# Key products of two chunks by pairs, two chunks of scores moved into the loop, and seven constant products ahead of it

## The chip, the cores and the metric

The kernel runs on one core of one Trainium2 chip. The metric is the device time of one execution in microseconds (us), as a median over runs. The profile is one further execution, recorded by the hardware profiler; it has a time of its own, and all rows below come from it. The engines are TensorE (PE in the rows; PEld is its weight load), VectorE (DVE), ScalarE (ACT), GpSimd (POOL) and SyncE (SP), which issues most DMAs.

## The reference, cut to what matters

A gated delta rule over 768 tokens for 4 batches of 8 heads (head size 48), and after it a mixture of 16 experts of which every token takes one:

```
k_n = k / (norm(k) + 1e-6)
for t in range(S):
    y[t]  = q[t] @ state                        # state: 48 x 48 for each batch and head
    v_old = k_n[t] @ state
    state = state + beta[t] * outer(k_n[t], v[t] - v_old)
x = y as 3072 rows of 384
group, then expert in the group, by argmax;  out = gate * (relu(x @ w1[e]) @ w2[e])
```

## The kernel before, in words

The 768 tokens are worked on in 24 chunks of 32 tokens (u = 0 to 23). Four chunks form a group. For each chunk `gram(u)` multiplies the chunk's keys by its keys and by its queries (one product for each pair of a batch and a head, in tiles of 48 rows by 32 columns) and ScalarE moves the results to SBUF: `gt` (keys by keys) for the group's inverse, `gq` (keys by queries, the raw scores) for the chunk. A product in f32 runs as two passes on TensorE, so 32 products stand as x32 in the order of instructions and as x64 in the trace; the transposes by the identity run as one pass each.

`inverse(g)` is the long part on VectorE: it turns `gt` over (L297), takes the norms, and inverts 32 by 32 triangles by some 90 small products and sums (L367, L373), then turns the result back (L401) and spreads it into `mtb` (L410 on VectorE, L412 on ScalarE). Only when `mtb` of group 0 is there can the first `w` be made (L488), and with it the recurrence begins.

The recurrence has one period for each chunk: `w_ps` (L488), state products `s_ps` (L499), the state copied back by ScalarE (`s_bd`, L505), output products `o_ps` (L513), then with the new state `a_ps` (L471) and `o_ps` of the next chunk (L480), a transpose of the finished rows (`t_ps`, L540), and `f` (L475), which `w_ps` of the next period reads. In each period `gram(u + 10)` stands between `w_ps` and `s_ps`, so that scores are made 10 chunks ahead (`LEAD = 10`). VectorE meanwhile goes on with the inverse of a later group; `scale(u + 2)` (L448) makes `vh` from the values `kv`.

The order of the work is written out by hand: within the attention part PE, DVE, ACT, POOL and SP each run their instructions in program order. Ahead of the loop the grams of chunks 0 to 9 are made. The first twelve steps are key products of chunks 0 to 3, both products of chunks 4 to 7, and query products of chunks 0 to 3; their PSUM homes change between a tile `g_ps` and two tiles `begin0`, `begin1`. Chunks 8 and 9 come after them, then two products of constants (L817) into the tile `s_ps`, which takes over the banks of `begin0` and `begin1`. Loads are timed by touches: ScalarE writes one column of a tile (L784), and the load of that tile on SP (L199 for keys and queries, L203 for values, L209 for constants) has to wait for it. The constants come in two parts; the second (`con`, 376.5 KB) holds the identity that the constant products read.

After period 23 the mixture of experts runs, 16 experts one after the other, bound by TensorE.

Of the kernel before, what the change touches and what calls it, by code (L numbers as in the profile page):

```python
# [9 lines left out]
F32 = mybir.dt.float32  # L10
I32 = mybir.dt.int32
AX = mybir.AxisListType
ALU = mybir.AluOpType
# [3 lines left out]
C = 32  # L17
RG = 4
# [48 lines left out]
def deltanet_then_moe(  # L67
# [109 lines left out]
    with ExitStack() as first:  # L177
# [59 lines left out]
        gts, raws, gqs, mts, norm, vhs, xs, turned_over = {}, {}, {}, {}, {}, {}, {}, set()  # L237
        begun_with = {}

        def gram(u, home=None, parts=(0, 1)):  # L240


            g, uu = divmod(u, RG)
            kqt = kqt_[u % NB]
            if uu == 0 and 0 in parts:
                gts[g] = wk.tile([128, C, RG, H], F32, tag="gt", name=f"gt{g}")
            g_ps = home
            if home is None:
                g_ps = ps.tile([128, 2, 512], F32, tag="g", name=f"g_ps{u}")
            g_out = g_ps.rearrange("p f (j x) -> p (f j) x", j=NP)[:, :, 0:2 * C].rearrange(  # L250
                "p h (a t) -> p h a t", a=2)
            for j in range(NP):
                for b in range(B):
                    for hh in range(2):
                        rows = slice(hh * 64, hh * 64 + D)
                        of = slice(parts[0], parts[-1] + 1)
                        nc.tensor.matmul(g_out[quads[b], hh * NP + j, of],  # L257
                                         lhsT=kqt[rows, 0, j, quads[b]],
                                         rhs=kqt[rows, of, j, quads[b]], start=True, stop=True,
                                         skip_group_check=True)  # L260
            if 0 in parts:
                nc.scalar.activation(
                    gts[g][:, :, uu].rearrange("p t h -> p h t"), g_out[:, :, 0, :],
                    ACT.Copy)
            if 1 not in parts:
                return None
            raws[u] = wk.tile([128, H, C], F32, tag="gq", name=f"gq{u}", bufs=LEAD + 1)
            nc.scalar.activation(raws[u], g_out[:, :, 1, :], ACT.Copy)
# [19 lines left out]
        def inverse(g):  # L288
# [30 lines left out]
                yield ROOTS  # L319
            else:  # L320
                nc.scalar.activation(r0, diag, ACT.Sqrt, bias=cut["tiny"])
                nc.scalar.activation(rooted, cut["tiny"], ACT.Exp)
                yield BEGUN
                nc.vector.reciprocal(r1, r0)
                yield
# [428 lines left out]
        def work(n):  # L754


            for task in behind:
                if held.get(task) not in (TURN, ROOTS, FACTOR):
                    due[task] = min(due[task] + n * 180 * rate[task], 4000.0)
            while True:  # L760
                able = [t for t in behind if held.get(t) is None and due[t] > 0]
                if not able:
                    break
                for task in able:
                    push(task)

        def allow(what):

            for task in list(behind):
                if held.get(task) is what:  # L770
                    push(task)
# [5 lines left out]
        with tc.manual_schedule(engines={mybir.EngineType.PE, mybir.EngineType.DVE,  # L777
# [3 lines left out]
            def begin(burst):  # L781

                for late, loads in burst:
                    nc.scalar.activation(late[:, 0:1], cut["tiny"], ACT.Copy)  # L784
                    for load in loads:
                        load()
# [1 line left out]
            first_grams = ([(u, (0,)) for u in range(RG)] + [(u, (0, 1)) for u in range(RG, 2 * RG)]  # L788
                           + [(u, (1,)) for u in range(RG)])
            for i, (u, parts) in enumerate(first_grams):  # L790
                gram(u, homes[i % len(homes)], parts)
                begin(bursts.get(i, ()))
                if i == RG - 1:
                    start(inverse(0), 1)
                    while BEGUN not in held.values():
                        work(2)
            allow(BEGUN)
            work(22)
            for _ in range(6):
# [3 lines left out]
            nc.gpsimd.tensor_copy(what[:, :, 0:2], cut["ids"].rearrange("p (u c) -> p u c", c=2))  # L803
            nc.gpsimd.tensor_copy(sel, ident.rearrange("p (g r) -> p g r", r=BL)[:, :, None, :]
                                  .to_broadcast([128, 4, 4, BL]))
            ahead = advance(0)
            next(ahead)
            for u in range(2 * RG, LEAD):
                gram(u, homes[u % len(homes)])
                begin(after_gram[u])  # L810
            begin_with.close()
            pst = first.enter_context(tc.tile_pool(name="ps_state", bufs=1, space=PSUM, side="right"))
            s_ps = pst.tile([128, B, 512], F32, tag="state", name="s_ps")
            s_at = s_ps[:, :, 0:H * D].rearrange("p b (j d) -> p b j d", j=NP)
            sorted_in.update(at=s_ps[:, 0, H * D:H * D + T * 3 * NE], begun=True)
            for n in (H * D, H * D):
                nc.tensor.matmul(s_ps[:, 0, 0:n], lhsT=ident, rhs=con[:, cols[1]:cols[1] + n],  # L817
                                 start=True, stop=True, skip_group_check=True)
            second = inverse(1)
            start(second, 0.95)  # L820
            while 0 not in mts:
                work(4)
                allow(ACT_STEP)
            mask(0)
            scale(1)
            allow(ROOTS)
# [1 line left out]
                work(2)  # L828
            allow(FACTOR)
            ahead_of = {u: [u + LEAD] if u + LEAD < NCH else [] for u in range(NCH + 1)}  # L830
            begun, x_in = set(), {}

            def add_rows(j, **how):
# [43 lines left out]
            for u in range(NCH + 1):  # L877
# [44 lines left out]
                if ending:  # L922
# [1 line left out]
                        allow(SORT)  # L924
                    found_0 = read_found()
                    gathered = gather_first(found_0)
                for v in ahead_of[u]:
                    gram(v)
                if ahead_of[u] or later or ending:
                    next(step)  # L930
# [9 lines left out]
                if not ahead_of[u] and not later and not ending:  # L940
                    next(step)
                next(step)
                if u < NCH - 1:
                    allow(PE_STEP)
                    allow(ACT_STEP)
# [383 lines left out]
```

## Time and profile before

| | |
|---|---|
| time, median of 3 runs | 493.04 us (491.14 to 493.22) |
| the profiled execution's own time | 492.32 us |
| its span, first to last instruction | 490.6 us |
| busy share of the span | PE 91%, PEld 86%, DVE 48%, ACT 40%, POOL 39% |
| mean granted TensorE clock | 0.992 |
| first `w_ps` begins | 42.01 us |
| `w_ps` of periods 1 and 2 | 49.71 and 56.82 us |

A timeline row reads: start in us, duration in us, engine, line, operation, output<-inputs, shape, xcount of instructions merged in the row, and in brackets how long the engine stood idle before it and what released it. "issue" as releaser means that nothing in the profile (no semaphore, no DMA) held the engine. A row with SPq is SP's queue issuing a DMA. In the DMA view, q1 carries the loads and stores of the program and q8 carries instructions.

### The profile page before, as it was taken

To read this page: it belongs to the slowest core of one execution; us is meant where nothing else is said; L and a number is where in the kernel's file an instruction comes from. 1 tells how busy PE (TensorE), PEld (TensorE's weight loads), DVE (VectorE), ACT (ScalarE), POOL (GpSimd) and SP (SyncE) were. 2 spreads that over 40 slices of the span, in tenths; PEclk is the share of its full clock that TensorE was granted. 3 is DMA by queue.
4 is the path that set the end of the run, shared out by engine and by line. 5 is a ranking of instruction groups with operands and counts; after the bars stand their busy time and mean duration, and the time that the engine had idled before them with its cause. 6 is when DMAs were issued, how large, how long until landed. Compare 5 with 4: busy or idle time off the path is not lost. (4 is left out here: it accounts for less than half of the span.)

```text
span 490.6 us, 18139 instructions
## 1 busy us (share of the span) xinstructions
PE 447.1 (91%) x7738; PEld 422.6 (86%) x7738; DVE 236.1 (48%) x866; ACT 193.8 (40%) x415; POOL 188.9 (39%) x328
## 2 busy tenths in 40 slices
PE   3437999999999999999999999999999999999992
PEld 3325888888888888889999999999999999999992
DVE  2998999999999994465201201220122012201210
ACT  3416978798887766641112112111211111111110
POOL 0041210634517132102466355544645465265122
PEclk9999999999999989999999999999999999999998
DMA  5466454454356533106978877967977797878830
GB/s 165 141 193 190 154 168 146 131 173 149 93 165 179 180 106 106 59 22 171 364 227 252 277 255 204 310 181 246 339 260 234 270 330 276 253 221 305 278 112 31
DMA packets 56741, 97.07 MB, mean 198 GB/s; under 512 B 18958, under 2 KB 41417, under 8 KB 56659
## 3 DMA queue, kind: packets, MB, share of 16 engines
q1 hardware_dynamic: 50739, 85.89, 54.7%
q0 software_dynamic: 5920, 10.00, 6.7%
q8 instruction: 62, 1.02, 0.9%
q14 instruction: 20, 0.16, 0.1%
HBM read 81.75 MB, written 14.27 MB: 196 GB/s over the span
## 5 line engine op out<-in xcount | busy, mean ns | idle before, releaser
L1113 PE MATMUL y_ps<-hid,w 128*128 128x224 f32 (+15 forms) x768 | 132.2, 331 | 0.0
L1113 PEld LDWEIGHTS y_ps<-hid,w 128*128 128x128 f32 x768 | 129.0, 190 | 0.3
L1094 PE MATMUL h_ps<-xt,w 128*128 128x232 f32 (+14 forms) x720 | 122.7, 330 | 0.0
L1094 PEld LDWEIGHTS h_ps<-xt,w 128*128 128x128 f32 x720 | 120.1, 190 | 0.3
L1066 POOL DMA_INDIRECT xq<-x_dram,from_q x92 | 87.6, 953 | 37.0 <-issue 24.6
L1097 ACT ACTIVATE hid<-h_ps 128x448 f32<-128x448 f32 (+15 forms) x64 | 32.1, 502 | 100.2 <-PE h_ps L1094 100.2
L1116 DVE COPY yt<-y_ps 128x232 f32<-128x232 f32 (+13 forms) x14 | 5.1, 366 | 135.3 <-PE y_ps L1113 135.3
L1125 POOL DMA_INDIRECT out_dram<-yo,to_i x32 | 34.0, 1064 | 91.3 <-DVE yo L1163 80.3
L1118 ACT ACTIVATE yt<-y_ps 128x224 f32<-128x224 f32 (+15 forms) x34 | 11.5, 337 | 116.6 <-PE y_ps L1113 116.6
L373 DVE TENSOR_TENSOR m<-m,below 128x16 f32<-128x16 f32 (+4 forms) x180 | 53.8, 299 | 0.3
L367 DVE TENSOR_TENSOR below<-m 128x16 f32<-128x16 f32 (+4 forms) x180 | 52.5, 293 | 0.1
L505 ACT ACTIVATE s_bd<-s_ps 48x768 f32<-48x768 f32 x46 | 37.0, 805 | 6.0 <-PE s_ps L499 5.1
L1163 DVE TENSOR_SCALAR yo<-yr,gate 128x384 f32<-128x384 f32 (+14 forms) x28 | 11.1, 415 | 48.5 <-DMA yr<-y_dram 39.8
L257 PE MATMUL g_ps<-kqt 48*32 48x64 f32 (+1 forms) x1216 | 19.4, 236 | 15.3 <-issue 7.9
L257 PEld LDWEIGHTS g_ps<-kqt 48*32 48x32 f32 x1216 | 14.8, 116 | 17.8 <-issue 12.9
L488 PEld LDWEIGHTS w_ps<-f,mtb 64*64 64x64 f32 x736 | 23.7, 137 | 5.6 <-ACT f L475 3.8
L412 ACT ACTIVATE mtb<-mt,con 128x256 f32<-128x256 f32 x39 | 28.2, 747 | 0.0
L488 PE MATMUL w_ps<-f,mtb 64*64 64x48 f32 x736 | 26.6, 222 | 1.5 <-ACT f L475 1.4
L499 PE MATMUL s_ps<-w,kv 32*112 32x96 f32 x736 | 24.5, 267 | 1.2 <-issue 0.5
L499 PEld LDWEIGHTS s_ps<-w,kv 32*112 32x112 f32 x736 | 20.5, 172 | 3.8 <-ACT w L492 0.8
L471 PE MATMUL a_ps<-s_bd,kqt 112*32 112x96 f32 x736 | 21.2, 253 | 2.3 <-ACT s_bd L505 1.3
L592 POOL TENSOR_TENSOR acc<-acc,hots 128x16 f32<-128x16 f32 x16 | 4.2, 261 | 47.1 <-DVE hots L590 46.1
(176 smaller groups left out, 577.2 us busy)
## 6 DMA issues: line engine op xcount, KB each, us to landing
w<-in_w_dram SPq DMA_DIRECT2D x29, 1536.0 KB, 8.8
kv<-in_kv_dram SPq DMA_DIRECT2D x24, 416.0 KB, 3.6
kqt<-in_kq_dram SPq DMA_DIRECT2D x20, 448.0 KB, 4.1
x_dram<-x SPq DMA_DIRECT2D x24, 192.0 KB, 2.3
w<-in_w_dram SPq DMA_DIRECT2D x24, 128.0 KB, 3.9
y_dram<-yq SPq DMA_DIRECT2D x36, 84.0 KB, 9.0
yr<-y_dram SPq DMA_DIRECT2D x14, 192.0 KB, 2.4
kqt<-in_kq_dram SPq DMA_DIRECT2D x8, 224.0 KB, 3.9
```

Of the source, the lines that this page charges most:

```text
L257: nc.tensor.matmul(g_out[quads[b], hh * NP + j, of], lhsT=kqt[rows, 0, j, quads[b]], rhs=kqt[rows, of, j, quads[b]], start=True, stop=True ...
L367: nc.vector.tensor_tensor(t, column.to_broadcast(like), row.to_broadcast(like), op=ALU.mult)
L373: nc.vector.tensor_tensor(to, to, t, op=ALU.add)
L412: nc.scalar.activation(mtb[:, rows, a], from_, ACT.Copy, scale=by)
L488: nc.tensor.matmul(w_ps[b, h], lhsT=mt[b, uu * H + (h % 2) * NP + h // 2], rhs=f[b, h], start=(h == 0), stop=True, skip_group_check=True)
L499: nc.tensor.matmul(s_at[0:KR, b, j], lhsT=k[quads[b], j, 0:KR], rhs=w[quads[b], 2 * j:2 * j + 2], start=(u == 0 and j == 0), stop=True, sk ...
L505: nc.scalar.activation(s_bd[rows, :, :, hh, :], s_at[rows, :, :, hh * D:(hh + 1) * D], ACT.Copy)
L1066: nc.gpsimd.indirect_dma_start(out=xq[:, g, :], out_offset=None, in_=x_dram[:, :].rearrange("n (q c) -> (n q) c", q=4), in_offset=bass.Ind ...
L1094: nc.tensor.matmul(h_ps[:, k], lhsT=w1[:, j, (f + k) * 128:(f + k + 1) * 128], rhs=xt[:, j, 0:R], start=(j == 0), stop=(j == DC - 1), skip ...
L1097: nc.scalar.activation(hid[:, f:f + 2], h_ps, ACT.Relu)
L1113: nc.tensor.matmul(y_ps, lhsT=w2[:, f, j * 128:(j + 1) * 128], rhs=hid[:, f], start=(f == 0), stop=(f == FC - 1))
L1125: put = nc.gpsimd.indirect_dma_start(out=out[:, :], out_offset=bass.IndirectOffsetOnAxis(ap=to[0:P, i:i + 1], axis=0), in_=yo[0:P, :], in_ ...
```

## The change: what it does

Three edits, and two small moves that go with them.

- `gram` has a new form `paired`, used for the first two steps (key products of chunks 0 and 1). Two batches are multiplied at once: 16 products of 64 by 64 in place of 32 of 32 by 32. Of each result the two blocks on the diagonal are wanted; ScalarE takes the even one times a mask into `part`, and VectorE adds the odd one times its mask into `gt`.
- The grams of chunks 8 and 9 leave the stretch ahead of the loop. Period 0 now makes chunks 8 and 9, period 1 makes chunks 10 and 11, each the first between `w_ps` and `s_ps` and the second after `o_ps`. From period 2 on it is as before.
- The two constant products become seven.
- The load of the exponential's table on ScalarE (the second ACT_TABLE_LOAD) moves from just after the square root to after all first grams.
- The touches that start the loads of chunks 10, 11, 12 and of the values of chunk 2 move behind the spreading of `mtb` of group 0. The first step of `advance(0)` moves with the products.

```diff
+            if paired:
+                for j in range(NP):
+                    for b in pairs:
+                        for hh in range(2):
+                            k = kqt[hh * 64:hh * 64 + D, 0, j, b]
+                            nc.tensor.matmul(g_out[b, hh * NP + j], lhsT=k, rhs=k, start=True,
+                                             stop=True, skip_group_check=True)
+                even, odd = cut["parity"][:, 0:1], cut["parity"][:, 1:2]
+                part = wk.tile([128, H, C], F32, tag="part", name=f"part{u}")
+                nc.scalar.activation(part, g_out[:, :, 0], ACT.Copy, scale=even)
+                nc.vector.scalar_tensor_tensor(
+                    gts[g][:, :, uu].rearrange("p t h -> p h t"), in0=g_out[:, :, 1], scalar=odd,
+                    in1=part, op0=ALU.mult, op1=ALU.add)
+                return
...
-                nc.scalar.activation(rooted, cut["tiny"], ACT.Exp)
...
-                gram(u, homes[i % len(homes)], parts)
+                gram(u, homes[i % len(homes)], parts, i < 2)
...
+            nc.scalar.activation(rooted, cut["tiny"], ACT.Exp)
...
-            for u in range(2 * RG, LEAD):
-                gram(u, homes[u % len(homes)])
-                begin(after_gram[u])
...
-            for n in (H * D, H * D):
+            for n in [H * D] * 7:
...
             while 0 not in mts:
                 work(4)
                 allow(ACT_STEP)
+            for u in range(2 * RG, LEAD):
+                begin(after_gram[u])
...
+            ahead_of.update({u: [2 * RG + 2 * u, 2 * RG + 2 * u + 1] for u in range(2)})
...
-                for v in ahead_of[u]:
+                for v in ahead_of[u][:1]:
                     gram(v)
...
                 next(step)
+                for v in ahead_of[u][1:]:
+                    gram(v)
```

On PE, from the last of the first twelve grams to the second `w_ps`, before (the number after a tile's name is the chunk; L257 is a gram):

```order
L257 MATMUL begin1_104<-kqt3_108 32x32 x32
L257 MATMUL begin1_104<-kqt8_113 32x64 x32
L257 MATMUL g_ps9_761<-kqt9_114 32x64 x32
L817 MATMUL s_ps_805<-con_66 128x384 x2
L488 MATMUL w_ps0_882<-vh0_715,mtb0_854 64x48 x16
L257 MATMUL g_ps10_903<-kqt10_115 32x64 x32
L499 MATMUL s_ps_805<-w0_899,kv0_117 112x96 x16
L513 MATMUL o_ps0_720<-w0_899,gqm0_857 64x48 x16
L471 MATMUL a_ps1_901<-s_bd_99,kqt1_106 32x96 x16
L480 MATMUL o_ps1_1048<-s_bd_99,kqt1_106 32x96 x16
L540 MATMUL t_ps0_1067<-con_66,x0_986 128x128 x3
L488 MATMUL w_ps1_1086<-f1_1046,mtb0_854 64x48 x16
```

and now (L271 is a gram, L826 the constant products, L501 `w_ps`):

```order
L271 MATMUL begin1_104<-kqt3_108 32x32 x32
L826 MATMUL s_ps_696<-con_66 128x384 x7
L501 MATMUL w_ps0_787<-vh0_687,mtb0_751 64x48 x16
L271 MATMUL g_ps8_809<-kqt8_113 32x64 x32
L512 MATMUL s_ps_696<-w0_804,kv0_117 112x96 x16
L526 MATMUL o_ps0_704<-w0_804,gqm0_762 64x48 x16
L271 MATMUL g_ps9_894<-kqt9_114 32x64 x32
L484 MATMUL a_ps1_806<-s_bd_99,kqt1_106 32x96 x16
L493 MATMUL o_ps1_990<-s_bd_99,kqt1_106 32x96 x16
L553 MATMUL t_ps0_1009<-con_66,x0_892 128x128 x3
L501 MATMUL w_ps1_1028<-f1_988,mtb0_751 64x48 x16
```

Two grams have left the stretch ahead of `w_ps0`, five constant products have come into it, and period 0 has one gram more, between `o_ps0` and `a_ps1`.

On ACT, from the last query scores of the first twelve grams to `w0`, before (L262 and L268 empty a gram, L784 is a touch, L412 spreads `mtb`):

```order
L268 ACTIVATE gq3_585<-begin1_104 128x256
L262 ACTIVATE gt2_721<-begin1_104 128x8x32
L268 ACTIVATE gq8_755<-begin1_104 128x256
L784 ACTIVATE kqt10_115<-con_66 128x1
L784 ACTIVATE kv2_119<-con_66 128x1
L262 ACTIVATE gt2_721<-g_ps9_761 128x8x32
L268 ACTIVATE gq9_795<-g_ps9_761 128x256
L784 ACTIVATE kqt11_116<-con_66 128x1
L784 ACTIVATE kqt0_105<-con_66 128x1
L412 ACTIVATE mtb0_854<-mt0_852,con_66 128x8x32
L492 ACTIVATE w0_899<-w_ps0_882 128x384
```

and now (L282 empties a gram, L797 is a touch, L425 spreads `mtb`, L810 is the moved table load):

```order
L282 ACTIVATE gq3_556<-begin1_104 128x256
L810 ACT_TABLE_LOAD
L810 ACTIVATE rooted_130<-con_66 128x1
L425 ACTIVATE mtb0_751<-mt0_749,con_66 128x8x32
L797 ACTIVATE kqt10_115<-con_66 128x1
L797 ACTIVATE kv2_119<-con_66 128x1
L797 ACTIVATE kqt11_116<-con_66 128x1
L797 ACTIVATE kqt0_105<-con_66 128x1
L505 ACTIVATE w0_804<-w_ps0_787 128x384
```

The spreading no longer stands behind four gram evictions, and the four touches stand behind it, together.

On ACT in period 0, from the first gram's eviction to `f` of the next period, before:

```order
L262 ACTIVATE gt2_721<-g_ps10_903 128x8x32
L268 ACTIVATE gq10_937<-g_ps10_903 128x256
L505 ACTIVATE s_bd_99<-s_ps_805 48x16x48 x2
L522 ACTIVATE x0_986<-o_ps0_720 128x384
L412 ACTIVATE mtb0_854<-mt0_852,con_66 128x8x32 x2
L475 ACTIVATE f1_1046<-a_ps1_901 128x384
```

and now (L518 copies the state, L535 the output, L488 makes `f`):

```order
L276 ACTIVATE gt2_808<-g_ps8_809 128x8x32
L282 ACTIVATE gq8_843<-g_ps8_809 128x256
L518 ACTIVATE s_bd_99<-s_ps_696 48x16x48 x2
L535 ACTIVATE x0_892<-o_ps0_704 128x384
L276 ACTIVATE gt2_808<-g_ps9_894 128x8x32
L282 ACTIVATE gq9_928<-g_ps9_894 128x256
L425 ACTIVATE mtb0_751<-mt0_749,con_66 128x8x32 x2
L488 ACTIVATE f1_988<-a_ps1_806 128x384
```

Two more evictions stand ahead of `f1`. In period 1 two stand ahead of `f2` in the same way. SP's and POOL's instructions stand in the same order as before.

## Rows read from the trace of the kernel before

**Rows 1.** The page's second part: the span in 40 equal slices of 12.3 us, the busy share of each in tenths.

```profile
PE   3437999999999999999999999999999999999992
...
DVE  2998999999999994465201201220122012201210
```

**Rows 2.** The timeline of PE from the start to period 2; counts are passes.

```profile
3.56 0.89 PE L257 MATMUL g_ps<-kqt 48*32 48x32 f32 x64 [3.56 <-DMA kqt<-in_kq_dram]
5.50 1.55 PE L257 MATMUL begin<-kqt 48*32 48x32 f32 x128 [1.05 <-DMA kqt<-in_kq_dram]
6.84 0.53 PE L257 MATMUL g_ps<-kqt 48*32 48x32 f32 x31
9.22 0.49 PE L257 MATMUL g_ps<-kqt 48*32 48x32 f32 x33 [1.84 <-issue]
11.18 1.97 PE L257 MATMUL begin<-kqt 48*32 48x64 f32 x94 [1.47 <-DMA kqt<-in_kq_dram]
14.51 0.85 PE L257 MATMUL begin<-kqt 48*32 48x64 f32 x34 [1.35 <-issue]
...
34.12 0.66 PE L257 MATMUL begin<-kqt 48*32 48x32 f32 x37 [5.27 <-issue]
...
38.34 0.88 PE L257 MATMUL g_ps<-kqt 48*32 48x64 f32 x38 [1.52 <-issue]
39.16 2.93 PE L817 MATMUL s_ps<-con 128*128 128x384 f32 x4
42.01 1.17 PE L488 MATMUL w_ps<-vh,mtb 64*64 64x48 f32 x32
...
44.48 0.33 PE L257 MATMUL g_ps<-kqt 48*32 48x64 f32 x12 [0.61 <-issue]
...
56.82 1.13 PE L488 MATMUL w_ps<-f,mtb 64*64 64x48 f32 x32
```

**Rows 3.** The DMA queues (queue and kind: packets, MB, share of 16 engines). First the page's row of q8 over the whole span, then the stretch 35.8 to 38.4 us (where q1 has no packet), then 38.3 to 41.8 us (where q8 has none), then 41.8 to 43.2 us.

```profile
q8 instruction: 62, 1.02, 0.9%
...
q8 instruction: 1, 0.02, 2.3%
...
q1 hardware_dynamic: 285, 0.95, 96.8%
...
q8 instruction: 1, 0.02, 4.9%
```

**Rows 4.** The timeline of VectorE: group 0's `gt` turned over, the first `vh`, group 0's result turned back, the last step ahead of the third `vh`, and that `vh`.

```profile
10.45 1.25 DVE L297 STREAM_TRANSPOSE m<-gt 128x1024 f32<-128x1024 f32 x1 [7.96 <-ACT gt L262]
...
28.95 0.56 DVE L448 TENSOR_TENSOR vh<-kv,normt 128x384 f32<-128x384 f32 x1
...
35.73 1.25 DVE L401 STREAM_TRANSPOSE mt<-m 128x1024 f32<-128x1024 f32 x1
...
41.16 0.21 DVE L373 TENSOR_TENSOR m<-m,corner 128x52 f32<-128x52 f32 x1
43.23 0.56 DVE L448 TENSOR_TENSOR vh<-kv,normt 128x384 f32<-128x384 f32 x1 [1.86 <-PE w_ps L488]
```

**Rows 5.** Loads and who reads them: SP's queue issues the values of chunk 0 and of chunk 2; POOL's first reading of the constants' second part; and, from the view of line L448 up to 60 us, the times at which VectorE's queue got through the two semaphore events of that line (the first of them is the one ahead of the third `vh`).

```profile
24.88 0.35 SPq L203 DMA_DIRECT2D kv<-in_kv_dram  x1
...
37.88 0.38 SPq L203 DMA_DIRECT2D kv<-in_kv_dram  x1
...
30.74 0.22 POOL L803 COPY what<-con 128x48 f32<-128x48 f32 x1 [15.30 <-DMA con<-in_const_dram]
...
L448 DVEq EVENT_SEMAPHORE  x2: 21/21/21, 42.8 to 51.3; - x2
```

**Rows 6.** The timeline of ScalarE: the second table load, the touches of chunks 6 and 7, the spreading ahead of the first `w`, and period 0 from its gram's eviction to `f`.

```profile
12.10 1.28 ACT L322 ACT_TABLE_LOAD   x1
...
14.20 0.28 ACT L784 ACTIVATE kqt<-con 128x1 f32<-128x1 f32 x2
...
40.17 0.73 ACT L412 ACTIVATE mtb<-mt,con 128x256 f32<-128x256 f32 x1
...
44.88 0.63 ACT L262 ACTIVATE gt<-g_ps 128x256 f32<-128x256 f32 x1 [0.64 <-PE g_ps L257]
45.30 0.43 ACT L268 ACTIVATE gq<-g_ps 128x256 f32<-128x256 f32 x1
...
47.50 0.49 ACT L522 ACTIVATE x<-o_ps 128x384 f32<-128x384 f32 x1
47.88 1.40 ACT L412 ACTIVATE mtb<-mt,con 128x256 f32<-128x256 f32 x2
49.19 0.47 ACT L475 ACTIVATE f<-a_ps 128x384 f32<-128x384 f32 x1
```

**Rows 7.** The stretch of the periods: the windows view from 45 to 170 us (stretch; its length; busy us and instruction count of PE, PEld, DVE, ACT, POOL; granted clock; DMA share; GB/s), what VectorE waited for between 36 and 200 us (total, times, longest), and three timeline rows where the last group's inverse ends.

```profile
45.00:170.00 125.00, 117.89 (x3932) 104.48 (x3929) 123.83 (x512) 105.81 (x209) 45.05 (x134) 1.00 0.50 152
...
DVE vh L448 <- PE w_ps L488: 1.9, 1, 1.9
...
178.56 1.25 DVE L401 STREAM_TRANSPOSE mt<-m 128x1024 f32<-128x1024 f32 x1
...
179.84 0.80 DVE L410 TENSOR_SCALAR mtb<-mt,con 128x256 f32<-128x256 f32 x2
...
180.97 1.62 PE L488 MATMUL w_ps<-f,mtb 64*64 64x48 f32 x32
```

More of the change, by code (lines that the diff above doesn't have):

```diff
@@ L238, in deltanet_then_moe, with gram @@
         begun_with = {}
-        def gram(u, home=None, parts=(0, 1)):
+        def gram(u, home=None, parts=(0, 1), paired=False):
             g, uu = divmod(u, RG)
@@ L805, in deltanet_then_moe @@
                                   .to_broadcast([128, 4, 4, BL]))
-            ahead = advance(0)
-            next(ahead)
-            for u in range(2 * RG, LEAD):
-                gram(u, homes[u % len(homes)])
-                begin(after_gram[u])
             begin_with.close()
@@ L815, in deltanet_then_moe @@
             sorted_in.update(at=s_ps[:, 0, H * D:H * D + T * 3 * NE], begun=True)
-            for n in (H * D, H * D):
+            for n in [H * D] * 7:
                 nc.tensor.matmul(s_ps[:, 0, 0:n], lhsT=ident, rhs=con[:, cols[1]:cols[1] + n],
                                  start=True, stop=True, skip_group_check=True)
+            ahead = advance(0)
+            next(ahead)
             second = inverse(1)
```

## The prediction

> **What bounds the kernel now.** I read the slices first, then the timeline of each engine up to 57 us, then the DMA view around TensorE's stops, then the waits of the periods.
>
> The slices show three parts [rows 1]: a beginning of some 40 us in which PE is a third to nine tenths busy, the periods up to 210 us with PE and VectorE both at nine tenths, and the experts with PE at nine tenths and VectorE nearly idle. In the last part PE's work follows without holes, so what the first 210 us gain or lose passes to the end unchanged.
>
> In the beginning the reader is to see two clocks. VectorE starts the inverse of group 0 at 10.45, after 7.96 us of idleness, and then runs without a hole until 41.37 (41.16 + 0.21), where it stands 1.86 us for the first `w_ps` [rows 4]. Its result `mt` is there at 36.98 (35.73 + 1.25). The first `w_ps` comes only at 42.01 [rows 2], because the spreading of `mtb` on ScalarE waits until 40.17 behind the evictions of chunks 8 and 9 [rows 6], and two constant products stand on PE until 42.0.
>
> The second thing is PE's stops with "issue" as releaser [rows 2]. The first comes after 64 + 128 + 31 = 223 passes, inside the gram of chunk 3. From there to the next are 33 + 94 = 127 passes, and so on every 127. In the stretch before the stop that ends at 38.34, the DMA queues moved nothing but one packet of q8 [rows 3]; over the span q8 moved 62 packets of 16 KB. So PE takes its instructions in pieces of 127 passes (254 of weights and products), and gets the next one some time after it has begun the last: 38.34 - 34.12 = 4.2 us later with the queues empty, 44.48 - 38.34 = 6.1 us later with q1 at 96.8%, where the packet came only after 41.8 [rows 2, 3]. In the periods PE passes 3932 in 125 us [rows 7], or 4.04 us for 127: the pace of the fetch with empty queues. VectorE waits for one `w_ps` in the whole stretch (1.9 us, the one at 43.23) [rows 7].
>
> [...]
>
> **The change, part by part.** All times are in the profiled execution (492.32 us, span 490.6, so 1.7 around it).
>
> *Pairs for chunks 0 and 1.* 32 passes of 64 by 64 in place of 64 of 48 by 32, twice. Chunks 0 to 3 then need 32 + 32 + 64 + 64 = 192 passes, under 223, so the stop inside chunk 3 falls into chunk 4, which waits for its keys until 11.18 anyway [rows 2]. Chunk 1 begins at 5.50 with its keys; a paired gram costs between 0.89 (the 64 passes of chunk 0) and 1.17 (32 passes of this shape in `w_ps`) [rows 2]. I take 0.9 to the next gram's start, 0.7 for chunk 2 (two grams in 1.55), 0.9 for chunk 3, then 0.6 for the eviction (as the 0.63 at 44.88 [rows 6]): 5.5 + 0.9 + 0.7 + 0.9 + 0.6 = 8.6. VectorE's start moves from 10.45 to 8.6, by 1.85. The added eviction on VectorE (128 by 256 elements, under the 0.56 of 128 by 384 [rows 4]) falls into its idle time before 8.6, and costs nothing.
>
> *The table load.* It held ScalarE for 1.28 from 12.10, while chunks 4 and 5 were to be evicted; the touches of 14.20 [rows 6] come at 13.4 without it and without the stop at 14.51. Each load behind them, the values of chunk 0 (issued 24.88) and the constants (there at 30.74) [rows 5], comes about 0.8 earlier. In its new place the load has 4 us of idle ScalarE. VectorE gets to its first `vh` 1.85 earlier, at 27.1. The values were there by 28.95, for no wait stands there [rows 4], so now by 28.15: it waits between 0 and 1.05. I take 0.25, near the row that shows none; `mt` is there 1.6 earlier, at 35.4.
>
> *VectorE's wait at the third `vh`.* The wait for `w_ps` goes, another takes its place. The touch of the values of chunk 2 now stands behind the spreading: 35.4 + 0.73 + 0.1, one issue of 0.4 ahead of it, 36.65 in all. Before, issue to landing took 42.8 - 37.88 = 4.9 [rows 5], behind the same load of chunk 10. So they land at 41.55. VectorE is there at 41.37 - 1.6 = 39.8, or up to 0.8 later, since group 1's norms, which POOL makes after it has the constants [rows 5], come only 0.8 earlier; I take 40.2 and a wait of 1.4. The third `vh` moves from 43.23 to 41.6: VectorE gains 1.6, and no more.
>
> *The first `w`.* The seven products need the constants (29.9) and the homes of the last grams; 14 passes. Four took 2.85 us (39.16 to 42.01) [rows 2], so 14 take 10.0 at that pace. [...] Between these I take 7.1, with a clock that rises on the way: `w_ps` at 37.0, bounds 36.3 (the spreading) and 39.9. That is 5.0 earlier than 42.01.
>
> *Two grams more in the periods.* On ScalarE 0.63 + 0.43 = 1.06 stand ahead of `f1`, and in period 1 ahead of `f2`; in period 0 that chain (47.50 to 49.19) has no hole [rows 6]. On PE each is 64 passes. Here the fetch decides. Before `w_ps` stand 718 passes now (900 before), so the piece that begins at pass 731 starts 13 passes into `w_ps` and has been fetched long before; the next, at 858, lies 12 passes into `o_ps0`, and is asked for only at about 37.0, just when the four loads of the moved touches go out together (four times 0.4 us from 36.3). Bounds: 37.0 + 4.2 = 41.2 with empty queues, 43.1 as between 38.34 and 44.48. I take 42.5, nearer to the loaded row. PE would need that piece at 39.9 (`w_ps` 1.1, gram 0.8, `s_ps` 1.0 after 37.0) and stops for 2.6. Then `o_ps0` ends at 43.2, chunk 9's gram at 44.0, its evictions at 45.1, the spreading (1.40) at 46.5, `f1` at 47.0. The piece at 985 comes at 46.7, 11 passes into L480; `w_ps` of period 1 at 47.6, against 49.71. The piece at 1112 (7 passes into `s_ps`) comes at 50.8, where PE stood ready at 49.6; the piece at 1239 (`a_ps2`) at 54.9. Then `a_ps2` 55.8, `f2` 56.35, `w_ps` of period 2 at 56.9, against 56.82 [rows 2].
>
> *The sum.* 5.0 gained at the first `w`, about 2.1 given back to the evictions of two grams and 3 to the fetch: 0 by period 2. From there PE runs the same instructions at the fetch's pace, and VectorE is 1.6 ahead of before, with nothing waiting for it. 492.32 becomes 492.3. The profiled execution lies 0.7 under the median of the three runs shown and inside them, so I state it as it is: 492.3.
>
> **The rivals.**
>
> *The lead is kept, and VectorE takes over.* If the pieces come with no loss beyond the old one, period 2 begins 5.0 - 2.1 = 2.9 earlier. VectorE, which has 1.6, then holds the end: its last `mtb` is spread at 180.64, and `w_ps` came at 180.97 [rows 7], so 0.33 of room: 1.6 + 0.33 = 1.9, or 490.4. For it: the fetch queue had room in several places. Against it: the four loads at once. [...]
>
> *The values of chunk 2 come early as well.* If they land by 40.2, VectorE gains 43.23 - 40.2 = 3.0, PE's 2.9 becomes the limit with 0.2 of the room, and the end goes to 489.2. Against it: 4.9 us for this load in the row.
>
> *Slower: the fetch stands behind all four loads.* Place: the piece at 858. q8's packet took its turn behind loads already in the queues (after 41.8 for two loads issued by 38.3 [rows 3, 5]). If it is asked for after the fourth load has gone out, at 37.5 or later (products that run longer do that too), it waits for four loads. In 3.5 us q1 moved 0.95 MB, about two such loads [rows 3], so four take some 6.5 from 37.4; and the piece was ready 2.7 after 41.8, so now at about 46.5, 4.0 later than taken. About 1 of it is lost in stops that would come anyway: 495.3. Against it: PE's queue may ask before `w_ps` itself runs.
>
> **How the numbers follow.** Lead spent, 492.3: 0.45. Lead kept, 490.4: 0.27. Early values, 489.2: 0.08. Slower, 495.3: 0.20. The range 489.8 to 495.4 leaves out most of the third and a tail of the last. What a measurement tells from no change is about 0.5%, 2.5 us. Faster by more: the early values, half of the lead kept, less a tail: 0.22. Slower by more: most of the last and a tail of the first: 0.18. Within: 0.60. The likeliest case's own range is 491.3 to 493.4.
>
> **What would show it.** VectorE's first turn at about 8.6; no "issue" stop in chunk 3. A wait of VectorE before the third `vh` with a DMA of `kv` as releaser, the `vh` at 41.6. `w_ps` at 37 and an "issue" stop of 2 to 3 us inside `o_ps` of period 0, with q8's packet late among four loads; `w_ps` of period 2 at about 56.9. If that stop is short and `w_ps` of period 2 comes near 54, the fetch was priced too high and the second case holds; if the stop lasts beyond 45, the last.

## The result and the profile after

The changed kernel takes 497.6 us (median of 20 runs, 493.7 to 503.51), the kernel before 493.13 us beside it (20 runs). The ratio is 1.0082, 95% interval 1.0055 to 1.0109: slower by 0.8%, some 4.0 us, where I forecast no change and a range that ended at 495.4. Ratios leave disturbed executions out and medians don't (five of the twelve of `e8_loads_two_and_two`, four of the change's twenty), so the two need not agree.

The profiled execution is the fastest of the twenty: 493.7 us, span 491.5, mean granted clock 0.991. It shows where the loss begins; the two further traces below (`e9_change_again`, `e12_change_third`) show its usual size.

VectorE in the changed kernel, with ScalarE's `mtb` as the last row; these lines stand 13 or 14 further down than before:

```profile
7.32 0.67 DVE L262 SCALAR_TENSOR_TENSOR gt<-begin,con,part 128x256 f32<-128x256 f32 x1 [1.53 <-ACT part L261]
8.89 1.25 DVE L311 STREAM_TRANSPOSE m<-gt 128x1024 f32<-128x1024 f32 x1 [0.91 <-ACT gt L276]
...
28.28 0.56 DVE L461 TENSOR_TENSOR vh<-kv,normt 128x384 f32<-128x384 f32 x1 [0.82 <-DMA kv<-in_kv_dram]
...
34.93 1.25 DVE L414 STREAM_TRANSPOSE mt<-m 128x1024 f32<-128x1024 f32 x1
...
44.18 0.56 DVE L461 TENSOR_TENSOR vh<-kv,normt 128x384 f32<-128x384 f32 x1 [3.69 <-DMA kv<-in_kv_dram]
...
36.21 0.77 ACT L425 ACTIVATE mtb<-mt,con 128x256 f32<-128x256 f32 x1 [5.99 <-DVE mt L414]
```

Against [rows 4] the reader sees the first turn 1.56 us earlier (8.89 for 10.45), `mt` 0.8 earlier, and then the third `vh` 0.95 later than before (44.18 for 43.23): the wait for `w_ps` is gone and a wait of 3.69 for the values has its place. `mtb` no longer stands behind two grams on ScalarE, it waits for `mt` alone.

PE from the constant products to period 2:

```profile
29.78 7.45 PE L826 MATMUL s_ps<-con 128*128 128x384 f32 x14 [1.50 <-DMA con<-in_const_dram]
...
37.16 1.14 PE L501 MATMUL w_ps<-vh,mtb 64*64 64x48 f32 x32
...
39.98 0.55 PE L526 MATMUL o_ps<-w,gqm 64*64 64x48 f32 x11
41.39 0.79 PE L526 MATMUL o_ps<-w,gqm 64*64 64x48 f32 x21 [0.86 <-issue]
...
43.58 0.49 PE L493 MATMUL o_ps<-s_bd,kqt 112*32 112x96 f32 x11
48.78 1.13 PE L493 MATMUL o_ps<-s_bd,kqt 112*32 112x96 f32 x21 [4.71 <-issue]
49.84 0.90 PE L553 MATMUL t_ps<-con,x 128*128 128x128 f32 x3
50.68 1.85 PE L501 MATMUL w_ps<-f,mtb 64*64 64x48 f32 x32
...
58.98 1.14 PE L501 MATMUL w_ps<-f,mtb 64*64 64x48 f32 x32
```

The first `w_ps` comes 4.85 us earlier than in [rows 2], period 1 a microsecond later, period 2 2.2 us later. The lead goes in one stop of 4.71 us, inside L493 (the next chunk's `o_ps`) after 11 passes, with "issue" as releaser. The `w_ps` behind it takes 1.85 us in place of 1.14. The DMA queues say what the stop waited for. The rows are of 37.5 to 38.1, of 38.1 to 40.1, of 40.1 to 46.1 (where q8 has no packet) and of 46.1 to 47.3 us; columns as in [rows 3].

```profile
q1 hardware_dynamic: 4, 0.02, 16.6%
...
q1 hardware_dynamic: 144, 0.52, 83.8%
q8 instruction: 1, 0.02, 5.9%
...
q1 hardware_dynamic: 531, 1.70, 100.6%
...
q1 hardware_dynamic: 117, 0.16, 39.5%
q8 instruction: 1, 0.02, 5.4%
```

SP's timeline gives the loads; the first row merges three issues, the last of them that of chunk 10's keys at 37.1.

```profile
28.16 9.26 SPq L199 DMA_DIRECT2D kqt<-in_kq_dram  x3
37.51 0.38 SPq L203 DMA_DIRECT2D kv<-in_kv_dram  x1
37.98 2.90 SPq L199 DMA_DIRECT2D kqt<-in_kq_dram  x2
40.99 0.37 SPq L203 DMA_DIRECT2D kv<-in_kv_dram  x1
```

The piece of instructions that begins at pass 858 (41.39) was fetched at 38.1 to 40.1, as the crowd began. The next one, as I read it, is asked for about when that piece begins; from 40.1 to 46.1 q1 keeps all 16 engines busy with what is left of the four loads and the values of chunk 3 behind them (1.70 MB), and only then does q8 get its packet through. PE's group of this line on the page reads:

```profile
L493 PE MATMUL o_ps<-s_bd,kqt 112*32 112x96 f32 x736 | 20.6, 249 | 5.2 <-issue 5.2
```

All but 0.5 of that line's 5.2 us of idleness is this one place. The next rows show the granted clock (columns as in [rows 7]):

```profile
35.20:48.80 13.60, 8.03 (x277) 6.23 (x276) 9.77 (x44) 8.06 (x18) 1.35 (x6) 1.00 0.63 181
48.80:52.30 3.50, 3.50 (x54) 2.89 (x56) 3.50 (x15) 1.11 (x2) 0.00 (x0) 0.51 0.37 102
52.30:59.00 6.70, 6.58 (x274) 5.78 (x271) 5.79 (x24) 5.85 (x12) 0.00 (x0) 1.00 0.34 116
```

Right behind the stop the granted clock is 0.51 for 3.4 us, against 1.00 ahead of it and behind it (the lower and the upper level in what follows), and PE gets through 54 passes where the next 6.7 us hold 274. Up to 35.2 us this view has no record of the clock and prints 1.00 (from 28 to 35.2 us as well); the level there has to be read from durations.

### The profile page after: what moved, and what is told of

The parts are those of the page before. It is cut to its first block, busy times and chain, and to the rows that moved or that the text cites. A ratio compares the mean times of both kernels' runs of the same rounds, so it can differ in the third digit from the quotient of the medians.

```text
span 491.5 us, 18033 instructions
## 1 busy us (share of the span) xinstructions
PE 450.4 (92%) x7684; PEld 424.5 (86%) x7684; DVE 237.6 (48%) x868; ACT 193.9 (39%) x415; POOL 188.9 (38%) x328
## 5 line engine op out<-in xcount | busy, mean ns | idle before, releaser
L1082 POOL DMA_INDIRECT xq<-x_dram,from_q x92 | 87.9, 955 | 34.6 <-issue 24.2
L518 ACT ACTIVATE s_bd<-s_ps 48x768 f32<-48x768 f32 x46 | 37.0, 805 | 5.3 <-PE s_ps L512 2.6
L425 ACT ACTIVATE mtb<-mt,con 128x256 f32<-128x256 f32 x39 | 28.2, 747 | 6.0 <-DVE mt L414 6.0
L501 PEld LDWEIGHTS w_ps<-f,mtb 64*64 64x64 f32 x736 | 24.0, 138 | 5.6 <-ACT f L488 3.6
L501 PE MATMUL w_ps<-f,mtb 64*64 64x48 f32 x736 | 26.8, 224 | 1.5 <-ACT f L488 1.4
L493 PE MATMUL o_ps<-s_bd,kqt 112*32 112x96 f32 x736 | 20.6, 249 | 5.2 <-issue 5.2
L526 PE MATMUL o_ps<-w,gqm 64*64 64x48 f32 x576 | 21.1, 220 | 1.8 <-issue 1.4
L605 POOL TENSOR_TENSOR acc<-acc,hots 128x16 f32<-128x16 f32 x16 | 4.3, 268 | 47.1 <-DVE hots L603 46.1
L271 PE MATMUL g_ps<-kqt 48*32 48x64 f32 (+1 forms) x1216 | 17.1, 231 | 5.2 <-DMA kqt<-in_kq_dram 3.4
```

The lines of the kernel that those rows point to most:

```text
L425: nc.scalar.activation(mtb[:, rows, a], from_, ACT.Copy, scale=by)
L501: nc.tensor.matmul(w_ps[b, h], lhsT=mt[b, uu * H + (h % 2) * NP + h // 2], rhs=f[b, h], start=(h == 0), stop=True, skip_group_check=True)
L518: nc.scalar.activation(s_bd[rows, :, :, hh, :], s_at[rows, :, :, hh * D:(hh + 1) * D], ACT.Copy)
L526: nc.tensor.matmul(o_ps[b, h], lhsT=gq[b, hq].rearrange("p a t -> p (a t)"), rhs=w[b, h], start=(u == 0 and h == 0), stop=True, skip_group ...
L1082: nc.gpsimd.indirect_dma_start(out=xq[:, g, :], out_offset=None, in_=x_dram[:, :].rearrange("n (q c) -> (n q) c", q=4), in_offset=bass.Ind ...
```

## The experiments

Theory F: the four loads (keys of chunks 10, 11, 12, values of chunk 2), issued together at 37 us, hold back PE's instructions and the values. Rival G: two more scores in periods 0 and 1 cost by themselves, wherever the loads are. Rival P: the seven products and the early clock do it. Each run of five rounds was set against the kernel before on the same chip. "Period 2" is its `w_ps` in that run's trace.

**e1_touch_early**: the change, its four loads ahead of the spreading of the first turn.

```
+            for u in range(2 * RG, LEAD):
+                begin(after_gram[u])
             begin_with.close()
...
-            for u in range(2 * RG, LEAD):
-                begin(after_gram[u])
             mask(0)
```

> The changed kernel with its four touches (loads of chunks 10, 11, 12 and the values of chunk 2) put back ahead of the spreading of mtb, right behind the last of the first twelve grams' evictions. Theory F (the four loads issued together at 37 us hold back PE's next pieces of instructions and the values): no stop of PE over 1.5 us in period 0 (4.7 us before the edit), VectorE's third vh at about 40.5 instead of 44.2, w_ps of period 2 at 55 to 57 instead of 59.0, and 3 to 6 us less than the changed kernel: a ratio of 0.992 to 1.000 to the kernel before. Theory G (two grams more in periods 0 and 1 cost what they cost, wherever the loads are): the stop stays or comes elsewhere, ratio 1.005 to 1.010. Theory P (the seven products, by warming the clock early and letting it fall again, cost the time): ratio 1.005 to 1.010, with the clock falling in period 1 as now.

Measured: 1.0037 (0.9996 to 1.0078), between the two. The wait for the values is gone, no stop is left inside L493, one of 1.69 us (1.5 at most expected) stands in period 0, and period 2 stands at 55.96:

```profile
42.70 1.19 PE L526 MATMUL o_ps<-w,gqm 64*64 64x48 f32 x21 [1.69 <-issue]
...
55.96 1.14 PE L501 MATMUL w_ps<-f,mtb 64*64 64x48 f32 x32
```

By the middle values the loads' place carries about half of the loss; the intervals of this run and of the change overlap, so the half itself is not shown. In its trace the start is 0.9 us ahead of before's.

**e2_two_products**: the change with `[H * D] * 2` in place of `[H * D] * 7`.

> The changed kernel with two constant products instead of seven. Theory F: the loads still go out together, the stop of 3 to 5 us in period 0 or 1 stays, w_ps may come at 36.3 but is not the one waited for; ratio 1.005 to 1.012. Theory G: the same. Theory P: without the five products the time comes back to that of the kernel before or below, 0.995 to 1.002.

Measured: 1.0082 (1.0041 to 1.0122), as the change. P falls. But the stop of 3 to 5 us that I expected is not there:

```profile
37.61 1.94 PE L501 MATMUL w_ps<-vh,mtb 64*64 64x48 f32 x32 [3.44 <-ACT mtb L425]
...
48.13 0.52 PE L493 MATMUL o_ps<-s_bd,kqt 112*32 112x96 f32 x11 [0.52 <-issue]
```

Without the products the clock rises only at 47.3, so period 0 runs at the lower level (`w_ps` takes 1.94) and lasts 11.5 us, and period 2 stands at 58.6. So the same loss comes with no stop over 0.52 behind the first `w`. I read it so that the products buy clock in period 0 and the stop takes it away again; that reading is not shown.

**e3_pairs_alone**: before, with the paired products of chunks 0 and 1 and nothing else.

> The kernel before with nothing changed but the paired key products of chunks 0 and 1 (the table load, the grams of chunks 8 and 9 and the two products stay). All three theories: VectorE's first turn at 8.6 to 8.9 instead of 10.45, third vh up to 1 us earlier, ratio 0.996 to 1.000. If the ratio is above 1.003, pairing itself costs, and F, G and P all lack something.

Measured: 0.9997 (0.9959 to 1.0036), VectorE's first turn at 8.84. The pairs neither cost nor gain, though period 2 comes at 55.45.

**e4_grams_alone**: before, with chunks 8's and 9's scores in periods 0 and 1 and the loads behind the spreading, nothing else.

```
-            for u in range(2 * RG, LEAD):
-                gram(u, homes[u % len(homes)])
-                begin(after_gram[u])
...
+            for u in range(2 * RG, LEAD):
+                begin(after_gram[u])
             mask(0)
...
+            ahead_of.update({u: [2 * RG + 2 * u, 2 * RG + 2 * u + 1] for u in range(2)})
```

> The kernel before with the grams of chunks 8 and 9 moved into periods 0 and 1 and the touches moved behind the spreading as in the change, but without pairs, with two products and with the table load in its old place. F and G: stop of PE in period 0 or 1 of 2 to 5 us, third vh after 43, ratio 1.004 to 1.012. P: no loss, ratio 0.996 to 1.002.

Measured: 1.0083 (1.0045 to 1.0121). This part alone loses as much as the whole change. Its two stops in period 0 are short of the 2 to 5 us expected:

```profile
41.72 0.45 PE L257 MATMUL g_ps<-kqt 48*32 48x64 f32 x10 [1.48 <-issue]
...
47.67 0.45 PE L257 MATMUL g_ps<-kqt 48*32 48x64 f32 x11 [0.86 <-issue]
```

The clock is at its lower level from 40.6 to 64.5, and period 2 comes at 64.28, the latest of all, for no greater loss.

**e5_all_but_grams**: the complement, with pairs, seven products and the moved Exp, and scores and loads where before has them.

> The changed kernel with the scores of chunks 8 and 9, and the loads that they release, back ahead of the first w, where the kernel before has them; the paired keys, the seven products and the moved Exp stay. F (four loads issued together behind the spreading) and G (two more scores in periods 0 and 1 cost wherever the loads are issued) both have nothing left to act here: ratio to before 0.994 to 1.000, no wait over 1.5 us for the values of chunk 2. A rival, P2 (the five more products raise the granted clock early, and a clock raised early falls again in the periods behind, as after's did at 48.88): mean granted clock of the runs below before's 0.9895 by 0.005 or more, ratio 1.003 to 1.010.

Measured: 1.0012 (0.9971 to 1.0053), at the upper end of what was expected. PE goes from the products into the periods without one stop over 0.4 us, and period 2 stands at 55.24. P2's drop in the runs' clock is not there either: mean 0.988, against 0.989 of before beside it.

**e6_loads_late_alone**: before, with only the loads moved behind the spreading.

```
                 gram(u, homes[u % len(homes)])
-                begin(after_gram[u])
...
+            for u in range(2 * RG, LEAD):
+                begin(after_gram[u])
             mask(0)
```

> The kernel before with one edit: the four loads that chunks 8's and 9's scores release (keys of chunks 10, 11 and 12, values of chunk 2) are issued behind the spreading of the first turn, as in the changed kernel; the scores stay ahead of the first w. F: the values of chunk 2 land past 44 us, the third chunk's vh waits 2 us or more, and a piece of PE's instructions comes late behind the loads: ratio 1.004 to 1.010. G: the scores are not moved, so 0.997 to 1.003, whatever the values' wait says.

Measured: 1.0066 (1.0026 to 1.0106). No score is moved, and the loss is of the same size. The late issue costs by itself, as F has it, but by another path: no late piece acts here. Period 0's gram of chunk 10 waits for its own keys, and the third `vh` behind that gram; the clock is at its lower level from 44.9 to 51.7. The change wants chunk 10's keys only in period 1, so this run does not show how much of the change's loss the loads' place makes.

```profile
44.32 0.96 PE L257 MATMUL g_ps<-kqt 48*32 48x64 f32 x64 [1.86 <-DMA kqt<-in_kq_dram]
...
45.38 0.56 DVE L448 TENSOR_TENSOR vh<-kv,normt 128x384 f32<-128x384 f32 x1 [4.58 <-PE g_ps L257]
```

**e7_grams_alone_loads_early**: e4 with the loads ahead of the spreading.

> The kernel before with the scores of chunks 8 and 9 in periods 0 and 1 and no other part of the change, and the four loads issued ahead of the spreading, so not with the late ones of e4_grams_alone (1.0083). F: without the late loads the loss goes, 0.997 to 1.003. G: the scores alone keep it, 1.005 to 1.010. If each carries half, 1.003 to 1.006, as e1_touch_early (1.0037) against the changed kernel (1.0082) has it.

Measured: 1.0095 (1.0057 to 1.0133), the number that I had set down for G. Its trace shows that the run doesn't isolate G:

```profile
33.83 0.66 PE L257 MATMUL begin<-kqt 48*32 48x32 f32 x37 [3.90 <-issue]
...
35.02 0.31 SPq L199 DMA_DIRECT2D kqt<-in_kq_dram  x1
35.43 0.38 SPq L203 DMA_DIRECT2D kv<-in_kv_dram  x1
35.90 0.85 SPq L199 DMA_DIRECT2D kqt<-in_kq_dram  x2
...
38.11 1.95 PE L488 MATMUL w_ps<-vh,mtb 64*64 64x48 f32 x32 [0.22 <-ACT mtb L412]
39.98 1.10 PE L257 MATMUL g_ps<-kqt 48*32 48x64 f32 x54
45.00 0.45 PE L257 MATMUL g_ps<-kqt 48*32 48x64 f32 x10 [3.92 <-issue]
```

Without pairs PE comes to a new piece at 33.83, just ahead of the four loads at 35.0, and the next piece follows 11.2 us later, inside period 0. The clock rises only at 51.3, so period 0 runs at the lower level. The expectation was mine and it was too simple. Nor did the early loads alone make the piece late: its packet came at 42.53, though q1 was at 25.9% from 34.6 to 36.2 and had room for one asked for at 33.83. In e4 too a packet came 6.1 us behind the beginning of the piece before it (33.02 and 39.14), with all queues empty from 36 to 39. So a piece is not always asked for when the one before it begins; when it is asked for stays open.

**e8_loads_two_and_two**: the change with the keys of chunk 10 and the values of chunk 2 early, the other two loads late.

> The changed kernel with the first two of the four loads (keys of chunk 10, values of chunk 2) issued ahead of the spreading and the other two (keys of chunks 11 and 12) where the change has them. F, if it is the wait for the values that costs: no wait for them at the third chunk's vh, and the ratio of e1_touch_early or better, 1.000 to 1.004. F, if it is PE's instruction piece behind loads issued at 37 us and later: keys of chunks 11 and 12 still stand ahead of it, stop of 3 us or more near 44 to 49 us, 1.004 to 1.009. G: no difference to the changed kernel, 1.005 to 1.010.

Measured: 0.9989 (0.9937 to 1.0040); the medians are 494.51 against 491.49 of before beside them, so I read no gain from it, and little else. In its trace (of a long execution, 498.42) the third `vh` has no wait for the values, the stop in L493 is 1.42 us in place of 4.71 (3 or more expected), and period 2 stands at 57.0.

**e10_one_gram_moved**: e1 with chunk 8's scores back ahead of the first `w`, and only chunk 9's in period 0.

> e1_touch_early (the change with its four loads issued ahead of the spreading, 1.0037) with chunk 8's scores back ahead of the first w and only chunk 9's in period 0, so half of what G speaks of. G in proportion to the moved scores: 1.000 to 1.003, and a first w about 2 us later than in e1 (37.6), with w_ps of period 2 no later than 56. If the scores are not what is left in e1 (its residue is granted clock whatever is moved): 1.003 to 1.007.

Measured: 1.0024 (0.9986 to 1.0061), median 491.8 against 491.71. Its first `w_ps` comes at 41.82, not the 39.6 expected: the 14 products took 7.16 from 34.73. Period 2 stands at 56.7 (56 at most expected), and no stop over 0.7 us lies in periods 0 and 1. The ratio is within what was expected if the scores cost, and its interval reaches into the other range as well. The trace says more: with the clock at its upper level throughout, period 0 with two scores takes 7.62 us (41.82 to 49.44), against 6.82 in e5 with one (41.31 to 48.13), and `w_ps` waits for `f`. First e10, then e5:

```profile
49.44 1.14 PE L501 MATMUL w_ps<-f,mtb 64*64 64x48 f32 x32 [0.70 <-ACT f L488]
...
48.13 1.13 PE L501 MATMUL w_ps<-f,mtb 64*64 64x48 f32 x32 [0.18 <-ACT f L488]
```

In these two traces a second score costs some 0.8 us, near the 1.06 of evictions that the prediction gave it.

**e9_change_again** and **e12_change_third**: the change, unchanged, for two more traces; **e11_before_again**: the same for before.

> The changed kernel once more, unchanged, for a second trace: the one at hand is of its fastest execution (493.7 of a median of 497.6). F: piece of PE's instructions after the one in o_ps0 comes late again, asked for behind the loads, stop of 3 us or more between 43 and 50 us, and the values of chunk 2 land past 43 us. Clock (most of the 4 us between that trace and the median is granted clock in stretches behind period 2, and not a longer start): w_ps of period 2 again between 57 and 61 us, and what the execution is longer than 493.7 by is matched by more time at 0.5 between 60 and 480 us at about 1.5 us for each stretch of 3.4. If the start varies instead: w_ps of period 2 past 61.

> The kernel before once more, unchanged: a second trace of it, to set its beginning against the changed kernel's two (w_ps of period 2 at 58.98 and 61.9). If the loss sits in the beginning, w_ps of period 2 is again at 55 to 58 us with no issue stop over 1 us behind the first w and no stretch at 0.5 between 42 and 60 us. If beginnings scatter in both kernels alike, it is at 58 or later, or a stretch at 0.5 lies there.

> The changed kernel for a third trace. If the loss sits in the beginning: w_ps of period 2 between 58.5 and 62.5, issue stops of 2.5 us or more in sum behind the first w, a stretch at 0.5 that begins between 42 and 53 us. If the first two traces were chance: w_ps of period 2 at 57.5 or earlier.

Measured: 496.68 (e9), 498.81 (e12) and 495.58 us (e11, before). `w_ps` of period 2 comes at 61.94 and 61.44 in the change, and at 56.95 in before; so the start carries the loss. F's part for e9 held in kind (a late piece again, the third `vh` at 43.74) and not in size, for its stops are 2.22 and 2.47 where 3 or more was expected; my other guess for it, that the missing microseconds are clock behind period 2, fell. The two stops of e9:

```profile
42.16 0.79 PE L526 MATMUL o_ps<-w,gqm 64*64 64x48 f32 x21 [2.22 <-issue]
...
48.19 1.18 PE L493 MATMUL o_ps<-s_bd,kqt 112*32 112x96 f32 x21 [2.47 <-issue]
```

The third trace of the change (e12):

```profile
40.01 0.79 PE L526 MATMUL o_ps<-w,gqm 64*64 64x48 f32 x21 [0.44 <-issue]
...
47.40 1.18 PE L493 MATMUL o_ps<-s_bd,kqt 112*32 112x96 f32 x21 [4.71 <-issue]
...
49.34 1.95 PE L501 MATMUL w_ps<-f,mtb 64*64 64x48 f32 x32
...
61.44 1.14 PE L501 MATMUL w_ps<-f,mtb 64*64 64x48 f32 x32
```

The stop is that of the first trace to the hundredth, and behind it the windows view shows what the fastest execution had been spared:

```profile
33.00:47.00 14.00, 9.23 (x277) 6.87 (x275) 10.55 (x42) 8.09 (x18) 3.56 (x10) 1.00 0.62 179
47.00:60.70 13.70, 13.30 (x312) 11.96 (x316) 10.31 (x44) 6.67 (x14) 0.15 (x1) 0.50 0.28 84
```

PE is busy for 13.3 of 13.7 us, at the lower clock level: period 1 takes 12.1 us (49.34 to 61.44) with one gram more (1.18), against 7.1 in [rows 2]. In e9 the clock is at that level from 43.8 to 60.9; the stop of 2.22 ends 1.6 us ahead of that and the one of 2.47 lies inside. Before's second trace has this in the same place:

```profile
42.01 1.95 PE L488 MATMUL w_ps<-vh,mtb 64*64 64x48 f32 x32
...
49.84 1.14 PE L488 MATMUL w_ps<-f,mtb 64*64 64x48 f32 x32 [0.19 <-ACT f L475]
...
56.95 1.14 PE L488 MATMUL w_ps<-f,mtb 64*64 64x48 f32 x32
```

**Taken together.** The change's three traces reach period 2 at 59.0, 61.9 and 61.4, before's two at 56.8 and 56.95: 3.9 us between the means, near the loss of 4.0. That so few traces meet it so closely is in part luck: as wholes these five executions differ by 2.4 us only. What comes behind period 2 (an execution's own time less the start of that `w_ps`) is 434.7, 434.7 and 437.4 in the change and 435.5 and 438.6 in before, higher where more stretches at the lower clock fall into it (0, 3.4 and 10.2 us of them; 3.4 and 13.7). Over all kernels the start sorts the ratios into two groups, with one trace for each variant: where period 2 comes by 57.1 (e1, e3, e5, e8, e10) they are 0.9989 to 1.0037; where it comes at 58.5 or later (the change, e2, e4, e6, e7) they are 1.0066 to 1.0095. Within a group it does not: 64.28 (e4) loses no more than 58.6 (e2), and a start ahead of before's gains nothing (55.24 in e5, 55.45 in e3).

## Why the prediction was wrong

*Pairs, right.* The first turn came at 8.89 for 8.6, without the stop in chunk 3, and alone it is worth nothing (e3). The added eviction took 0.67 where it was put under 0.56, and hid all the same.

*Table load, right in its cost, half in what follows.* It hides at 28.72. The first `vh` waited 0.82 for the values where I took 0.25, so `mt` was there 0.8 earlier and not 1.6.

*The third `vh`, right in kind, wrong in size.* The wait for the values took the place of the one for `w_ps`, as said, but the load went out at 37.51 for 36.65 and took some 6.6 us (to 44.1) in the crowd of four, not the 4.9 of [rows 5]: 44.18 for 41.6. VectorE lost 0.95 where I gave it 1.6.

*The first `w`, right.* 37.16 for 37.0, with seven products in 7.4 us for the 7.1 taken. The 7.1 was a choice under the 10.0 that the pace of the four products gives [rows 2]; how far under, no row of before shows. In its place the run shows passes of 847 ns at first and 486 at the end (L826: 486/847/977), seven of them in 4.82 us and the other seven in some 2.6, which I read as a clock that rose in their course. That the 7.1 came out so near is in part luck.

*Two grams more in the periods: here it failed.* The step reads "the next, at 858 ... I take 42.5" and "the piece at 985 comes at 46.7". I put the crowd of loads on the piece at 858 and gave the next one an open road, 4.2 us behind it. The order was the other way round. The packet of piece 858 came soon after piece 731 began, 13 passes into `w_ps`, and early among the loads (38.15, 39.49 and 37.33): the piece began at 41.39, 42.16 and 40.01 in the three traces, by the 42.5 taken or before it. The packet of piece 985 came behind the loads (46.16, 45.70 and 44.70): the piece began at 48.78, 48.19 and 47.40, which is 7.4, 6.0 and 7.4 us behind its forerunner, and 2.1, 1.5 and 0.7 later than the 46.7 of the sum. The last rival had this mechanism (the packet behind all four loads), at the wrong piece, with 0.20.

*A term that was not in the sum: the clock.* "1.1, gram 0.8, `s_ps` 1.0" and all periods behind were reckoned at the durations of [rows 2], which ran at the upper level (`w_ps` in 1.13 to 1.17). In the change the clock fell at 48.88, 43.80 and 47.01, each time during a stop or within 2 us behind one, and stayed low for 3.4, 17.1 and 13.7 us. `w_ps` of period 2, put at 56.9, came 2.1, 5.0 and 4.5 late. In the fastest execution, with 3.4 us at the lower level, that is no more than the piece was late; in the two others 3.5 and 3.8 us of it came behind the piece, where period 1 ran at the lower level. So in two traces of three the clock, which the sum put at nothing, is the larger part. The rival's 495.3 was too little for the median as well: it had the stop and not what came behind it. That the stops bring the clock down is argued from this order of events, from e1, whose clock fell at 42.89, right behind its stop of 1.69, and from e5 and e10, which have no stop over 0.7 us in periods 0 and 1 and no fall before 100 us; e3 and e2 speak against a firm rule: e3 has a stop that ends at 45.49 after 1.87 us and no fall until 68.25, e2 has a fall at 54.12 with no stop over 0.52 behind the first `w`. No run held the clock apart from the stops.

*"From there PE runs the same instructions at the fetch's pace", right.* Behind period 2 the two kernels take the same time within the clock's scatter.

Why did such stops not cost this before? They cost another thing: 5.27 and 1.52 us of them [rows 2] lay ahead of the first `w_ps`, and it came at 42.01 though `mt` was there at 36.98. Behind it the recurrence met only one more, of 0.61, up to period 2. The change took the two scores out from behind those stops and brought the first `w` forward by 5 us, and with it PE came 5 us earlier to pieces that still had to be fetched, and to keys and values that still had to be loaded. What the step from one piece to the next costs differs by place: here one cost 4.71 us, with q1 at 100.6% ahead of its packet, and in e5 none cost over 0.4 from the products to period 2.

*What stays open.* With early loads (e1) 0.4% is left, with an interval that reaches to no change; e10 has 0.2%. How the loss divides into late pieces, late loads and lower clock was not separated: e7, which was to part the scores from the loads, met a late piece and the lower clock again. In what is left of e1 the start is early, and 439.7 us come behind period 2, with 10.2 at the lower level. No variant beat the kernel before beyond its interval.

## What to carry to other kernels

Before bringing the first step of a chain forward, ask for each thing that it and the next steps need whether it comes forward as well: here the loads and the instruction pieces did not, and a lead of 5 us became a loss of 4. From 40.1 to 46.1 us q1 moved 1.70 MB of loads and q8 had no packet: count the passes to each piece (127 here [rows 2]), look up when its packet came, and try bursts of loads outside the time between that and the need (with the four loads early, e1 had no stop over 1.69). Price a stop of TensorE, or an earlier start, with the clock level that the work then runs at (`w_ps` took 1.95 us at 0.50 and 1.14 at 1.00 in e12), and look at more than one trace: the fastest execution showed half of this loss.

## What was not expected of the hardware

An instruction packet of 16 KB came 4.8 us after the piece before it began (piece at 41.39, packet from 46.16) while q1 moved 1.37 MB, against some 1.1 us where the queues had room (e1: begun 42.70, packet from 43.85). Full queues did not always hold it up so long: in e2 it came 2.0 us after (43.46 and 45.42) with q1 at 102.7%. One stop of PE took the same to the hundredth in two traces (4.71; 2.47 in the third), while the clock behind it stayed at its lower level for 3.4 us in the one execution and 13.7 in the other. And the kernel before scatters as well, but later: its second trace spent 13.7 us at the lower level behind 100 us, against 3.4 in the first, and was 3.3 us longer.
